# Gate and up weights in runs of 2 KB: another cut of two weight matrices into the same pieces

## The chip, the core and the metric

The kernel runs on one core of a Trainium2 chip. The metric is the device time of one execution in microseconds (us). Three runs of the kernel before gave 324.64, 325.95 and 326.41 us, a median of 325.95.

## The reference, cut to what matters

```python
x = A_x                                             # 2048 x 512, bf16
x = x + _A_ref(_layernorm(x), A_wqkv, A_wo)         # 32 heads of 16, causal window of 256
x = x + _B_ref(_layernorm(x), B_w_r, B_w_gate, B_w_up, B_w_down)
x = x + _A_ref(_layernorm(x), A_wqkv, A_wo)
x = x + _B_ref(_layernorm(x), B_w_r, B_w_gate, B_w_up, B_w_down)

def _B_ref(x, w_r, w_gate, w_up, w_down):           # C = 1: one row of 2048 goes through the MLP
    r = x @ w_r
    idx = argsort(-r)[:, :1]
    x_sel = x[idx]                                  # 1 x 512
    y = (silu(x_sel @ w_gate) * (x_sel @ w_up)) @ w_down        # 512 -> 1792 -> 512
    return x + scatter(idx, y * sigmoid(r[idx]))
```

So each of the two layers has an attention over 2048 rows and an MLP of a single row. For that row the gate and up products are matrix times vector: 512 x 1792 weights each, of which 128 x 128 blocks are loaded into TensorE as weights and multiplied with one column.

## The kernel before, in words

The kernel is a list of operations (`S.add`, `S.dma`), each with an engine, the tiles it reads and writes, an assumed duration and a priority. `Sched.schedule` (line 189) plays this list through once, at build time, and so fixes the order of every engine's instructions. The chip then runs the five orders with semaphores between them; an engine never overtakes in its own order.

Two rules of the planner matter here. The attention's matmuls on TensorE (PE) carry a `seq` and run in the order of that number. All other PE operations are "loose" (line 248): one of them is put ahead of the next fixed operation when it can start no later than that one and has a lower priority number, or when it fits before it. And a DMA is taken to land a fixed while after its issue, plus its bytes and the bytes of the DMAs issued before it (lines 355 to 357); the planner does not know into how many runs a DMA falls. SyncE (SP) issues nearly all DMAs, in one order.

The sequence is cut into 16 tiles of 128 rows per layer. While the attention of a layer runs, the row for the MLP is chosen from the first 11 tiles (layer 0) or 10 tiles (layer 1) (`select`), fetched from DRAM and normed into `XST`, a tile of 128 x 4: row `4p + kc` of the 512 sits in partition `p`, column `kc`. Then come, in both layers:

- `load_mlp` (line 1277): 21 pieces of weights of 256 KB, 1024 elements per partition. Pieces 0, 2, ... 12 are gate, 1, 3, ... 13 are up, 14 to 20 are down. Each piece goes to a home (`spots`, lines 1511 and 1528) in a tile that is free for the moment: `MW`, `XI`, `QT` and others. In layer 0 the homes of pieces 11 to 17 are those of pieces 2 to 9, so these loads wait until a gate-up step has read the old piece (line 1523): pieces 11 and 12 after step 1, 13 and 14 after step 2, 15 and 16 after step 3, 17 after step 4. A load's priority is that of its step.
- `mlp_gu` (line 1316): seven gate-up steps. Step `c` takes pieces `2c` and `2c + 1` and makes blocks `2c` and `2c + 1` of the 14 blocks of 128 outputs, for gate and up: 32 matmuls of one column, each block a sum over four `kc` that opens and closes by itself. All steps write one PSUM bank. Their priorities fall with `c` in layer 0 (`gu0` = -5.834 per step) and rise with `c` in layer 1 (`gu1` = 2.222); no step depends on another, but steps 5 and 6 of layer 0 need pieces 11 to 13.
- `mlp_act` (line 1339) and `mlp_down` (line 1350): silu, the product, and 56 matmuls with the down pieces; then the row is put back by a DMA. In layer 0 the second layer's loads of the rows wait for that.

The gate and up weights lie in DRAM as 512 rows of 1792. Before, a piece is 256 columns of all rows: per partition four runs of 256 elements (512 bytes), each of another row. A home in `QT` holds a piece as four runs of 256 elements that lie apart; in every other home the piece's 1024 elements of a partition are one run.

Of the kernel before, what the change touches and what calls it, by code (L numbers as in the profile page):

```python
# [505 lines left out]
FULL, HALF = 1, 2  # L506
# [19 lines left out]
class Builder:  # L526
# [750 lines left out]
    def load_mlp(self, c, where, at):  # L1277

        S = self.S
        buf, keys = self.home(where)  # L1280
        wk = ["piece%s%d" % where] if where[0] == "w" else keys
        deps = set()
        if where[0] == "w":
            for x in keys:
                deps.add(S.last_writer[x])
                deps.update(S.readers.get(x, ()))
        deps.add(S.groups[-1].ops[0])
        if c < 14:
            n = 256 * (c // 2)
            src = (self.B_w_gate, self.B_w_up)[c % 2].rearrange("(p kc) n -> p kc n", p=128)[:, :, n:n + 256]  # L1290
            dst = buf if where[0] == "qt" else buf.rearrange("p (kc n) -> p kc n", kc=4)
        else:
            n = 2 * (c - 14)
            src = self.B_w_down.rearrange("(j p) n -> p j n", p=128)[:, n:n + 2, :]
            dst = buf.rearrange("p (j n) -> p j n", j=2)
        S.dma("sp", lambda e: e.dma_start(dst, src), writes=wk, nbytes=256 * 1024, name="ld_mw", prio=at, extra_deps=deps)
        self.pieces[c] = (dst, wk)
# [18 lines left out]
    def mlp_gu(self, L, c, at, ate):  # L1316

        S = self.S
        S.base = at
        NF = self.NF  # L1320
        if c == 0:
            self.GUG = S.group("x")
        G = self.GUG
        ps = [self.pieces[2 * c + u] for u in range(2)]

        def gu(e):
            r = None
            for u in range(2):
                for j in range(2):
                    k = NF * u + 2 * c + j  # L1330
                    for kc in range(4):
                        r = e.matmul(self.PS[:, G.bank, k:k + 1], lhsT=ps[u][0][:, kc, 128 * j:128 * j + 128], rhs=self.XST[:, kc:kc + 1],  # L1332
                                     start=(kc == 0), stop=(kc == 3))
            return r
        S.add("pe", gu, reads=["xst"] + ps[0][1] + ps[1][1], banks=[0], group=G, dur=16 * 27 + 150, instrs=32, mode=FULL, name="gateup", prio=at + POS["gp%d" % L])
        if c == 6:
            S.add("dve", lambda e: e.tensor_copy(out=self.GU[:], in_=self.PS[:, G.bank, 0:2 * NF]), banks=[0], group=G, writes=["gu"], dur=110, name="evgu", prio=ate)

# [1213 lines left out]
```

## Time and profile before

| | |
|---|---|
| median of 3 runs | 325.95 us (324.64 to 326.41) |
| profiled execution | 326.61 us, its span 324.9 us |
| PE busy | 305.1 us (94%), 7315 matmuls |
| PE weight loads | 222.0 us (68%) |
| DVE, ACT, POOL busy | 272.4, 272.9, 143.7 us |
| DMA queue of SP and ACT | 44.78 MB in the span, 58.3% of 16 engines |

Times of rows are microseconds from the span's start unless marked ns. PE is TensorE's matmuls, PEld its weight loads, which run beside them; DVE is VectorE, ACT ScalarE, POOL GpSimd, SPq the DMA issues of SyncE. The busy share of PE is an upper bound, since the ends of pipelined matmuls are modelled. The granted TensorE clock is 0.998 of full speed over the span.

### The profile page before, as it was taken

To read this page: it belongs to the slowest core of one execution; us is meant where nothing else is said; L and a number is where in the kernel's file an instruction comes from. 1 tells how busy PE (TensorE), PEld (TensorE's weight loads), DVE (VectorE), ACT (ScalarE), POOL (GpSimd) and SP (SyncE) were. 2 spreads that over 40 slices of the span, in tenths; PEclk is the share of its full clock that TensorE was granted. 3 is DMA by queue.
4 is the path that set the end of the run, shared out by engine and by line. 5 is a ranking of instruction groups with operands and counts; after the bars stand their busy time and mean duration, and the time that the engine had idled before them with its cause. 6 is when DMAs were issued, how large, how long until landed. Compare 5 with 4: busy or idle time off the path is not lost.

```text
span 324.9 us, 16648 instructions
## 1 busy us (share of the span) xinstructions
PE 305.1 (94%) x7315; PEld 222.0 (68%) x7377; DVE 272.4 (84%) x728; ACT 272.9 (84%) x313; POOL 143.7 (44%) x322
## 2 busy tenths in 40 slices
PE   8978999999999999999998999999999999989995
PEld 3735677677766776777776567677677767767773
DVE  7987998999797878799877899879788687888793
ACT  8599999999889899988357999898989998999621
POOL 6280348688656170414733457351304222313441
PEclk9999999999999999999999999999999999999999
DMA  7826312627447968736694477989967546554502
GB/s 240 272 78 131 71 34 68 166 44 166 79 126 185 152 172 128 171 75 178 197 152 106 124 155 198 214 211 211 272 167 216 151 146 135 168 121 103 118 18 58
DMA packets 86546, 46.95 MB, mean 145 GB/s; under 512 B 52420, under 2 KB 80708, under 8 KB 86468
## 3 DMA queue, kind: packets, MB, share of 16 engines
q1 hardware_dynamic: 85380, 44.78, 58.3%
q8 instruction: 59, 0.97, 1.3%
q10 hardware_dynamic: 1088, 1.05, 1.0%
q14 instruction: 19, 0.16, 0.3%
HBM read 24.78 MB, written 13.43 MB: 118 GB/s over the span
## 4 chain that ended last, share of the span: by engine, by line
PE 77%; ACT 11%; DVE 4%; issue 3%; DMA 3%; SPq 0%; POOL 0%; POOLq 0%
PE PS L981 16%; PE PS L839 15%; PE PS L861 15%; PE PS L1047 14%; ACT PT L959 11%; PE PS L1052 9%; PE PS L1013 3%; DMA vd<-VN 2%; PE PS L666 2%; PE PS L1332 1%; PE PS L1408 1%; DVE KBD L931 1%; PE PS L1372 1%; DVE ON L1071 1%; DMA VBD<-vd 1%
## 5 line engine op out<-in xcount | busy, mean ns | idle before, releaser
L959 ACT ACTIVATE PT<-PS 128x1024 bf16<-128x1024 f32 (+4 forms) x284 | 257.6, 989 | 34.1 <-PE PS L981 33.1
L981 PE MATMUL PS<-QT,KBD 64*128 64x256 bf16 (+4 forms) x1024 | 82.3, 265 | 1.9 <-issue 0.9
L1137 POOL TENSOR_TENSOR XR<-XR,MHALF 128x1 f32<-128x1 f32 x32 | 18.9, 589 | 139.2 <-DVE XR L1136 133.8
L861 PE MATMUL PS<-XNT,WQKV 128*128 128x256 bf16 x480 | 62.6, 274 | 1.6 <-DVE ON L1071 0.8
L981 PEld LDWEIGHTS PS<-QT,KBD 64*128 64x128 bf16 x1024 | 35.6, 94 | 36.2 <-issue 14.2
L1047 PE MATMUL PS<-VBD,PT 128*128 128x68 bf16 x1488 | 55.2, 196 | 1.7 <-DMA VBD<-vd 1.3
L861 PEld LDWEIGHTS PS<-XNT,WQKV 128*128 128x128 bf16 x480 | 42.6, 98 | 17.5 <-issue 7.1
L1047 PEld LDWEIGHTS PS<-VBD,PT 128*128 128x128 bf16 x1488 | 50.8, 97 | 5.5 <-issue 3.9
L1052 PEld LDWEIGHTS PS<-VBD,PT 64*128 64x128 bf16 x2784 | 40.4, 93 | 3.4 <-ACT PT L959 1.6
L1052 PE MATMUL PS<-VBD,PT 64*128 64x34 bf16 x2784 | 41.6, 175 | 0.9 <-ACT PT L959 0.5
L992 DVE TENSOR_TENSOR PT<-PT,MSK 128x512 bf16<-128x512 bf16 x64 | 28.4, 444 | 7.9 <-ACT PT L959 7.6
L839 PE MATMUL PS<-WQKV,XNT 128*128 128x512 bf16 x99 | 26.4, 379 | 4.9 <-issue 2.9
L1071 DVE TENSOR_TENSOR ON<-PS,RD 128x256 bf16<-128x256 f32 x64 | 26.9, 420 | 1.5
L874 DVE CAST KTN<-PS 128x512 bf16<-128x512 f32 x30 | 20.6, 687 | 8.2 <-PE PS L861 8.2
L839 PE MATMUL PS<-WO,OT 128*128 128x512 bf16 x90 | 24.3, 379 | 3.3 <-issue 2.5
L931 DVE TENSOR_SCALAR KBD<-KTN,M 128x1024 bf16<-128x1024 bf16 x60 | 26.3, 488 | 0.4
L1069 DVE RECIPROCAL RD<-PS 128x16 f32<-128x16 f32 x64 | 16.1, 252 | 10.4 <-PE PS L1052 7.6
L1138 DVE SCALAR_TENSOR_TENSOR JUNK<-XR,WR 128x512 bf16<-128x512 f32 x32 | 23.6, 738 | 0.7
L923 DVE CAST VN<-PS 128x512 bf16<-128x512 f32 x30 | 20.6, 685 | 4.0 <-PE PS L839 3.9
L874 DVE CAST QT<-PS 128x512 bf16<-128x512 f32 x28 | 19.2, 684 | 5.0 <-PE PS L861 4.6
L1134 DVE BATCH_NORM_STATS2 ST6M<-XR 128x6 f32<-128x512 f32 x32 | 21.8, 681 | 0.0
L839 PEld LDWEIGHTS PS<-WQKV,XNT 128*128 128x128 bf16 x128 | 10.6, 97 | 13.5 <-issue 2.7
(149 smaller groups left out, 343.2 us busy)
## 6 DMA issues: line engine op xcount, KB each, us to landing
scr<-XR SPq DMA_DIRECT2D x12, 516.0 KB, 3.7
vd<-VN SPq DMA_DIRECT2D x16, 272.0 KB, 3.9
VBD<-vd SPq DMA_DIRECT2D x128, 34.0 KB, 2.8
XR<-scr SPq DMA_DIRECT2D x8, 512.0 KB, 4.6
XI<-in_B_w_down_dram SPq DMA_DIRECT2D x7, 256.0 KB, 3.2
out_dram<-OUTB SPq DMA_DIRECT2D x7, 256.0 KB, 4.2
XI<-in_A_x_dram SPq DMA_DIRECT2D x6, 256.0 KB, 7.4
MW<-in_B_w_up_dram SPq DMA_DIRECT2D x6, 256.0 KB, 5.2
```

The source lines that it names most:

```text
L839: r = e.matmul(self.PS[:, G.bank, 0:n], lhsT=lhs(j), rhs=rhs(j), start=(j == 0), stop=(j == 3))
L861: r = e.matmul(self.PS[:, G.bank, 256 * u:256 * u + 256], lhsT=self.WQKV[:, j, c:c + 128], rhs=XNT[:, kb, 2 * h:2 * h + 2, j, :], start=(u ...
L874: S.add("dve", lambda e: e.tensor_copy(out=dst, in_=src[:, G.bank, :].rearrange("p (s t) -> p s t", s=2)), banks=[0], group=G, writes=keys ...
L931: S.add("dve", lambda e, h=h: e.tensor_scalar(out=self.KBD[:, k2, :, :, 32 * h:32 * h + 32].rearrange("p s b k -> p (s b) k"), in0=src, sc ...
L959: return e.activation(out=out, in_=i, func=ACTF.Exp, scale=0.25)
L981: r = e.matmul(self.PS[:, G.bank + x, W * u:W * u + n], lhsT=self.KBD[rows, k2, s, 4 * (T % 2) + b, :], rhs=self.QT[rows, s, q0:q0 + n], s ...
L992: S.add("dve", lambda e: e.tensor_tensor(out=P, in0=P, in1=m, op=ALU.mult), reads=["msk"], writes=["pt%d_%d" % ((4 * T + b) % 12, 2 * sp + ...
L1047: r = e.matmul(o, lhsT=self.PT[:, c:c + 128], rhs=self.VBD[:, v, kb % 4, :, 2 * s + a, :], start=isfirst and kb == blocks[0] and g == 0, s ...
L1052: r = e.matmul(self.PS[:, G.bank + x, 34 * g:34 * g + 34], lhsT=self.PT[rows, c:c + 128], rhs=self.VBD[rows, v, kb % 4, 2 * x:2 * x + 2, 2 ...
L1071: S.add("dve", lambda e: e.tensor_tensor(out=o, in0=acc()[:, :, :, 0:16], in1=rd.unsqueeze(3).broadcast_to([128, 2, 8, 16]), op=ALU.mult), ...
L1134: S.add("dve", lambda e: e.bn_stats(out=self.ST6M[:, km, :], in_=x), reads=[xk], writes=["st6m#%d" % km], dur=600, name="bnst2", prio=ag)
L1138: S.add("dve", lambda e: e.scalar_tensor_tensor(out=self.JUNK[:], in0=x, scalar=1.0, in1=self.WR16[:], op0=ALU.mult, op1=ALU.mult, accum_o ...
```

## The change

A piece now is, per partition, a run of 1024 elements out of the 7168 that the four rows of a partition make together (they are adjacent in DRAM). With 14 blocks of 128 columns in a row, piece number `c` (of gate or of up) holds the blocks `8c` to `8c + 7` of the 56 blocks of all four rows, so that a step has eight blocks of gate and eight of up, of one `kc` or of two. The number of matmuls, their shapes, the homes and the bytes stay the same.

The sums over `kc` now run across steps. So one matmul of a layer, the first of step 0, opens the bank (`start`), all others add to it or write where nothing was written yet, and each step depends on the step before it (`extra_deps`).

```diff
         if c < 14:
-            n = 256 * (c // 2)
-            src = (self.B_w_gate, self.B_w_up)[c % 2].rearrange("(p kc) n -> p kc n", p=128)[:, :, n:n + 256]
+            n = 1024 * (c // 2)
+            src = (self.B_w_gate, self.B_w_up)[c % 2].rearrange("(p kc) n -> p (kc n)", p=128)[:, n:n + 1024].rearrange("p (a n) -> p a n", a=4)
             dst = buf if where[0] == "qt" else buf.rearrange("p (kc n) -> p kc n", kc=4)
...
             for u in range(2):
-                for j in range(2):
-                    k = NF * u + 2 * c + j
-                    for kc in range(4):
-                        r = e.matmul(self.PS[:, G.bank, k:k + 1], lhsT=ps[u][0][:, kc, 128 * j:128 * j + 128], rhs=self.XST[:, kc:kc + 1],
-                                     start=(kc == 0), stop=(kc == 3))
+                for j in range(8):
+                    kc, k = divmod(8 * c + j, NF)
+                    k += NF * u
+                    r = e.matmul(self.PS[:, G.bank, k:k + 1], lhsT=ps[u][0][:, j // 2, 128 * (j % 2):128 * (j % 2) + 128], rhs=self.XST[:, kc:kc + 1],
+                                 start=(c == 0 and u == 0 and j == 0), stop=(c == 6 and u == 1 and j == 7), skip_group_check=True)
             return r
-        S.add("pe", gu, reads=["xst"] + ps[0][1] + ps[1][1], banks=[0], group=G, dur=16 * 27 + 150, instrs=32, mode=FULL, name="gateup", prio=at + POS["gp%d" % L])
+        self.gu_ix = S.add("pe", gu, reads=["xst"] + ps[0][1] + ps[1][1], banks=[0], group=G, dur=16 * 27 + 150, instrs=32, mode=FULL, name="gateup", prio=at + POS["gp%d" % L],
+                           extra_deps=[self.gu_ix] if c else [])
```

## Rows read from the trace of the kernel before

**Rows 1.** Page, part 4: chain that ended last, shares of the span by engine.
```profile
PE 77%; ACT 11%; DVE 4%; issue 3%; DMA 3%; SPq 0%; POOL 0%; POOLq 0%
```

**Rows 2.** Waits of PE, whole span: engine, line, releaser: total us, times, longest us.
```profile
PE PS L1047 <- DMA VBD<-vd: 1.3, 1, 1.3
```

**Rows 3.** Chain that ended last, whole span and from 296: start, us, what.
```profile
22.49 2.13 DMA VBD<-vd
...
296.60 0.38 PE PS L1332 x16
```

**Rows 4.** The same chain, stretch of 150 to 200.
```profile
155.49 1.98 PE PS L1332 x80
...
160.63 0.98 PE PS L861 x8
...
164.99 0.88 PE PS L1332 x32
...
171.24 0.85 issue
...
174.69 9.31 ACT PT L959 x10
```

**Rows 5.** Stretches: PE, PEld, DVE, ACT, POOL busy, clock, DMA share, GB/s.
```profile
170.00:172.20 2.20, 1.35 (x79) 1.06 (x72) 1.34 (x5) 1.78 (x2) 1.91 (x5) 1.00 0.21 36
...
210.00:240.00 30.00, 29.29 (x743) 21.57 (x749) 23.86 (x59) 27.41 (x30) 10.73 (x24) 1.00 1.02 235
```

**Rows 6.** Line 1332, gate-up matmuls: ns min/median/max, first and last start us.
```profile
L1332 PE MATMUL PS<-XST,MW x88: 163/163/177, 156.1 to 298.8; 128*128 128x1 bf16 x88
...
L1332 PE MATMUL PS<-XST,XI x72: 163/163/178, 155.3 to 313.6; 128*128 128x1 bf16 x72
...
L1332 PE MATMUL PS<-XST,QT x64: 163/163/178, 155.5 to 313.8; 128*128 128x1 bf16 x64
```

**Rows 7.** Timeline of PE's weight loads, 150 to 175: start, us, what.
```profile
155.25 0.32 PEld L1332 LDWEIGHTS PS<-XST,XI 128*128 128x128 bf16 x8 [0.26 <-issue]
...
156.10 0.87 PEld L1332 LDWEIGHTS PS<-XST,MW 128*128 128x128 bf16 x32
156.90 0.47 PEld L1332 LDWEIGHTS PS<-XST,QT 128*128 128x128 bf16 x16
...
164.92 0.27 PEld L1332 LDWEIGHTS PS<-XST,QT 128*128 128x128 bf16 x8 [0.21 <-issue]
165.12 0.67 PEld L1332 LDWEIGHTS PS<-XST,MW 128*128 128x128 bf16 x24
```

**Rows 8.** Timeline of SP's DMA issues, 130 to 161: start, us, what.
```profile
143.00 0.33 SPq L950 DMA_DIRECT2D VBD<-vd  x1
...
155.95 1.43 SPq L1296 DMA_DIRECT2D XI<-in_B_w_down_dram  x3
157.44 0.58 SPq L1296 DMA_DIRECT2D MW<-in_B_w_up_dram  x1
...
159.33 0.82 SPq L1296 DMA_DIRECT2D MW<-in_B_w_gate_dram  x1
160.25 1.03 SPq L950 DMA_DIRECT2D VBD<-vd  x2
```

**Rows 9.** Line 1296, issues of the weight loads: ns min/median/max, first and last start.
```profile
L1296 SPq DMA_DIRECT2D XI<-in_B_w_down_dram x7: 390/403/1123, 143.8 to 248.3; - x7
...
L1296 SPq DMA_DIRECT2D MW<-in_B_w_gate_dram x5: 571/598/820, 92.0 to 207.6; - x5
L1296 SPq DMA_DIRECT2D QT<-in_B_w_up_dram x5: 546/594/1354, 101.2 to 243.7; - x5
```

**Rows 10.** DMA issues in 155 to 161: count, KB each, median us to landing.
```profile
XI<-in_B_w_down_dram SPq DMA_DIRECT2D x3, 256.0 KB, 3.0
MW<-in_B_w_up_dram SPq DMA_DIRECT2D x2, 256.0 KB, 5.4
```

**Rows 11.** DMA view, whole span: packets by size.
```profile
DMA packets 86546, 46.95 MB, mean 145 GB/s; under 512 B 52420, under 2 KB 80708, under 8 KB 86468
```

## The prediction, made before the result was known

> **What bounds the kernel now.** I read the chain of waits first. Three quarters of it are TensorE's own instructions, a ninth is ScalarE, and DMA has 3% [rows 1]. Then the waits of TensorE: there are three for a DMA in the whole trace, all in the start-up; the one shown lies on the chain at 22 us [rows 2, 3], long before the first gate or up weight is asked for at 92.0 us [rows 9]. From there to the end no matmul waits for a transfer. Even where the DMA share is highest, 1.02 with 235 GB/s in 210 to 240 us, PE is busy 29.29 of 30 us [rows 5]. So the reader is to see a kernel that is bound by the order and the number of PE's instructions, with DMA beside it.
>
> The stretch that the change touches most is 155 to 175 us, between the layers. There the chain runs over the gate-up steps themselves: 80 matmuls in 1.98 us, then 32 in 0.88 us. It has one hole of 0.85 us at 171.24 in which PE waited for nothing that the profile shows, and at 174.69 it goes over to ScalarE, which had been waiting for scores [rows 4]. What is lost or won by PE before 174.69 therefore reaches the end of the kernel one to one, until another slack swallows it.
>
> **The change part by part.** The sum is made against the profiled execution, 326.61 us with a span of 324.9; the median of the runs is 0.66 us below it, and I take that off at the end.
>
> *PE's work.* Gate-up is 88 + 72 + 64 = 224 matmuls of one column in both layers, 163 ns each in the median [rows 6], and by the diff there are 224 of the same shape after (7 steps of 16, two layers). The opening of the bank is a flag on a matmul, no instruction. Cost: 0.
>
> *The transfers.* 28 pieces are loaded. A piece of four runs costs SP 0.57 to 0.60 us, a down piece, which is two runs of 1 KB per partition, 0.40 us [rows 9], a quarter of V with 128 runs 0.33 us [rows 8]. A piece of 128 runs should cost 0.33 to 0.40 us, so SP gains 0.17 to 0.27 us per piece. Eight of the 28 have their home in `QT`, where the written side stays four runs of 512 bytes; if the shorter side counts, those gain nothing, and SP saves 20 x 0.17 = 3.4 us at the least, 28 x 0.27 = 7.6 us at the most. None of it is on the path: the first layer's loads that need no freed home are issued from 92.0 us on for a step at 155.49 [rows 4, 9], and the second layer's end at 243.7 us for a step at 296.60 [rows 3, 9]. The cover is 52 us there. What could be quicker behind a shorter queue are V loads and transposes, and PE waits for none of them now. Value: 0; bounds below.
>
> The Trainium skill (DMA: Bandwidth & Descriptors, Specifications) puts the smallest transfer at full rate at 512 bytes, by which the old runs were already good and the change would not move more bytes per microsecond. The same page (Why small descriptors are slow) counts three cycles for each packet on top of one per 32 bytes: an estimate from it is 4 x 19 = 76 cycles before and 67 after, 12% less. The rows mix this with the queue: in the same stretch three down pieces landed in 3.0 us and two up pieces, queued behind them, in 5.4 [rows 10]. By either the sum stays, since nothing waits; by the first, the slower rival below is likelier.
>
> *The chain of steps.* In layer 1 the steps' priorities already rise with the step, so nothing moves. In layer 0 they fall, and the order of homes in the trace says so: `XI` and `QT` first (step 4), then `XI` (3), `MW` (2 and 1), `QT` (0), then after 8 us `QT` and `MW` (5 and 6) [rows 7]. The chain turns the five round: 0, 1, 2, 3, 4. As a burst they cost what they cost now, 1.98 us. What moves is what waits for them: SP's loads into freed homes. Now the first, the three into `XI`, leave at 155.95, when step 4 has read, and the last, piece 12 into `MW`, at 159.33 [rows 8]. After, the first is piece 11, when step 1 has read: 32 matmuls of 24.7 ns after 155.49, that is 156.28, and about 0.06 us for the signal as now, so 156.34. Behind it SP takes by priority 13, then 15, 17, 16, 14, and 12 last. All seven go 0.39 us later at the start, but three of them are of the new kind and 0.2 us cheaper each, so that the V loads behind them, now at 160.25 [rows 8], leave within 0.3 us of that, and piece 12 no later than now.
>
> *Step 5 moves forward.* It needs pieces 10 and 11 only. By its own rule the planner counts piece 11 as landed 4.35 us after its issue (0.62 for the issue, 0.3, 0.93 for 256 KB, 2.4, and 0.1 for the signal; this says where it puts the step, not what the chip takes), that is at about 160.7 on the trace's scale. Step 5 has a lower priority number than any fixed operation there, so it goes into PE's order at that place, just ahead of or behind the projection at 160.63 [rows 4], four microseconds before its place of now. Step 6 waits for piece 12 and stays near 165. So the pair of steps, 32 matmuls in 0.88 us, is split. Against the rate in the burst (32 x 24.7 ns = 0.79 us) a group that stands alone costs 0.09 us more; one more group costs +0.09 us. Downstream, `mlp_act` and the down matmuls hang on step 6 and keep their place, or slip by a few matmuls: 0 to 0.4 us (half of the 0.85 us that a group of such small matmuls now takes at 165), and I take 0.
>
> *The hole of 0.85 us.* It stands in the stretch 170 to 172.2, in which the DMA share is 0.21 and 36 GB/s move [rows 5]. A queue that is nearly empty is not made quicker by fewer packets, so I leave the hole where it is: 0, with -0.85 as its other end.
>
> Sum: 0 + 0 + 0.09 + 0 + 0 = +0.1 us on 326.61, or 326.05 on the scale of the median: I say 326.0. What a measurement of this kernel can tell from no change is about 0.5%, 1.6 us: under 324.3 is faster, over 327.6 slower.
>
> **The rivals.**
>
> *Faster: the emptier DMA queues reach PE after all.* PE's instructions come over DMA too, and if such fetches stood behind packets of the weights, the small pauses of PE in the loaded stretches would shrink. Speaking for it: a pause with no cause shown. Against it: that pause falls into an empty stretch, and the fullest one has PE idle for only 0.71 of 30 us [rows 5]. Price at most: the 0.85, and 0.71/30 over the 53 us in which the second layer's pieces are loaded, 1.25 us; together -2.1, so 323.9 us. The Trainium skill (Runtime: NRT & Kernel Launch, Instruction fetch mechanics) says that an engine fetches blocks of 256 instructions over a DMA queue of its own, mostly hidden; the row at 170 us agrees that weights are not what it waits for.
>
> *Slower: PE stands before step 5.* PE's order is fixed, so if piece 11 has not landed when step 5 is up, the projection and the scores behind it all wait, and ScalarE after them. It decides at 160.63 - 156.34 = 4.3 us after the issue. For it: the two up pieces into `MW` landed after 5.4 us in just this stretch; then PE stands 5.4 + 156.34 - 160.63 = 1.1 us. Against it: those stood behind three others, while piece 11 would be the first in its queue, and the three at the head now took 3.0 us [rows 10]. Step 5 would also set 32 small instructions right behind a dense stretch of PE, where a second hole like that at 171.24 can open, 0.85 us. Price: 1.1 + 0.85 + 0.09 = +2.0, so 328.0 us.
>
> *The runs don't become 2 KB.* The source is written as four times 256 elements in the diff. If that is how it is carried out, the packets stay what they are, only the chain acts, and the time is the forecast's, 326.0, with piece 11 a little later.
>
> **How the numbers follow.** No change, with the case that the runs stay short: 0.56, its own range 325.1 to 327.3. The faster rival 0.20, at 323.9. The slower rival 0.17, at 328.0. The planner plays the whole list again, and an order tipped elsewhere by step 5's place can go either way: 0.02 faster, 0.05 slower. So faster 0.22, same 0.56, slower 0.22, and a range that leaves out the outer part of both rivals, 324.1 to 328.1.
>
> **What would show it.** Packets: 14,336 of the 86,546 [rows 11] are runs of the 28 pieces (512 each); all in 2 KB would leave 75,794, the `QT` pieces excepted 78,866, and 86,546 would mean that nothing was joined. The issue of a piece into `MW` or `XI` should take 0.33 to 0.40 us. In layer 0 the homes should come in the order `QT`, `MW`, `XI`, `QT`, and 16 of the matmuls should start at about 160.5, without idle time of PE ahead of them that ends with a DMA. The hole near 171 should still be there. I would be wrong if that hole goes or a second one comes, if step 5 waits, or if the second layer's stretches, where only the loads differ, change their length.

## The result, and the profile after

The changed kernel takes 329.0 us in the median of 12 runs (326.36 to 331.46), the one before 326.48 beside it (324.45 to 327.81, 12 runs): a ratio of 1.0068, 95% interval 1.0038 to 1.0097. The ratio leaves out one run of after, the 331.46, that lies over 1.5% above its fastest. The change is slower, by 0.7%, where none was forecast; 329.0 lies above the range.

What was said of the loads came out. The page of the kernel after has the packets of the case in which the `QT` pieces stay short, 78,866 against the 86,546 of before [rows 11]:

```profile
DMA packets 78866, 46.95 MB, mean 143 GB/s; under 512 B 52420, under 2 KB 70468, under 8 KB 78788
```

The place where the time went shows in the chain of waits of after, from the burst of gate-up steps on (start, us, what). It answers to [rows 4]. (A gate-up step is 16 matmuls, eight of gate and eight of up, so the 80 are five steps; the 32 in the words on the kernel count the weight loads too.)

```profile
154.48 1.98 PE PS L1332 x80
...
157.07 1.23 PE PS L861 x8
...
158.47 1.39 PE PS L1052 x96
159.85 0.52 PE PS L1332 x16
160.38 1.79 issue
162.16 0.56 PE PS L981 x8
162.72 1.82 PE PS L861 x8
164.54 0.22 issue
164.76 1.48 PE PS L839 x3
...
166.52 1.47 PE PS L1047 x24
...
169.20 0.48 PE PS L1332 x16
...
175.25 0.98 PE PS L861 x8
```

Step 5 (159.85) starts about where the prediction put it, and PE does not wait for it. Behind it PE stands still for 1.79 us with no releaser. And the projection, 0.98 us at 160.63 in [rows 4], takes 1.82 us. The windows of after show why (PE busy, clock, DMA share, GB/s): the granted clock fell to half, 1.2 GHz, even before the hole.

```profile
154.00:158.00 4.00, 3.82 (x94) 0.96 0.58 137
158.00:162.00 4.00, 2.38 (x118) 0.50 1.00 320
162.00:166.00 4.00, 3.61 (x19) 0.50 1.41 179
166.00:170.00 4.00, 4.00 (x71) 0.76 0.00 0
```

Before has a short hole at the same place, which the rows ahead of the prediction do not list. Its row in the chain of before, with that of the projection behind the down matmuls:

```profile
161.61 0.29 issue
...
172.48 0.98 PE PS L861 x8
```

From the burst's start to that projection (at 172.48 before, at 175.25 after) it is 16.99 us before and 20.77 after, +3.78. By the rows: the hole +1.50; instructions stretched by the half clock +2.58 (L861 +0.25 and +0.84, L1052 +0.17, L839 +0.67, L981 +0.07, L1047 +0.58); the pause at 164.54 +0.22; step 5 alone +0.12 (0.52 + 0.48 - 0.88); the split of a group in the down steps +0.09; and the hole of 0.85 at 171 is gone. That makes 3.66. From there to the end the two agree within 0.3 us; up to the burst after was 1.01 us ahead, so the spans differ by 2.6 and not by 3.8. The burst starts anywhere between 153.8 and 155.6 in the profiles of this document, so I read nothing into that. And this execution has the lowest mean clock of after's 12 (0.984; the others have 0.988 to 0.995), so the half clock is likely to cost less than 2.58 in most of them.

SP's timeline of after says what else moved (start, us, issue), against [rows 8]:

```profile
152.56 2.83 SPq L950 DMA_DIRECT2D VBD<-vd  x4
155.49 0.38 SPq L1187 DMA_DIRECT2D scr<-XR  x1
155.96 0.86 SPq L1296 DMA_DIRECT2D MW<-in_B_w_up_dram  x2
156.92 1.49 SPq L1296 DMA_DIRECT2D XI<-in_B_w_down_dram  x3
```

The store of a row tile to `scr`, 258 KB, now leaves ahead of the seven loads. Before, it left behind them:

```profile
163.85 0.43 SPq L1187 DMA_DIRECT2D scr<-XR  x1
```

### The profile page after: what moved, and what is told of

The parts are those of the page before. It is cut to its first block, busy times and chain, and to the rows that moved or that the text cites. A ratio compares the mean times of both kernels' runs of the same rounds, so it can differ in the third digit from the quotient of the medians.

```text
span 327.5 us, 16648 instructions
## 1 busy us (share of the span) xinstructions
PE 307.1 (94%) x7315; PEld 223.4 (68%) x7377; DVE 272.1 (83%) x728; ACT 272.6 (83%) x313; POOL 143.7 (44%) x322
## 2 busy tenths in 40 slices
DMA packets 78866, 46.95 MB, mean 143 GB/s; under 512 B 52420, under 2 KB 70468, under 8 KB 78788
## 4 chain that ended last, share of the span: by engine, by line
PE 77%; ACT 13%; DVE 5%; issue 3%
PE PS L861 16%; PE PS L981 16%; PE PS L839 15%; PE PS L1047 14%; ACT PT L959 12%; PE PS L1052 9%; PE PS L1013 3%; PE PS L1332 1%; PE PS L1409 1%; DVE KBD L931 1%; PE PS L1373 1%; DVE VBD L680 1%; PE PS L1108 1%; DVE ST L772 1%; DVE ON L1071 1%
## 5 line engine op out<-in xcount | busy, mean ns | idle before, releaser
L981 PE MATMUL PS<-QT,KBD 64*128 64x256 bf16 (+4 forms) x1024 | 82.4, 266 | 3.1 <-issue 1.8
L861 PE MATMUL PS<-XNT,WQKV 128*128 128x256 bf16 x480 | 63.6, 277 | 1.6 <-DVE ON L1071 0.8
L981 PEld LDWEIGHTS PS<-QT,KBD 64*128 64x128 bf16 x1024 | 35.8, 94 | 38.2 <-issue 15.0
L1047 PE MATMUL PS<-VBD,PT 128*128 128x68 bf16 x1488 | 55.8, 197 | 1.3 <-ACT PT L959 1.1
L861 PEld LDWEIGHTS PS<-XNT,WQKV 128*128 128x128 bf16 x480 | 43.0, 98 | 17.9 <-issue 7.3
L1047 PEld LDWEIGHTS PS<-VBD,PT 128*128 128x128 bf16 x1488 | 51.4, 98 | 5.2 <-issue 3.5
L1052 PEld LDWEIGHTS PS<-VBD,PT 64*128 64x128 bf16 x2784 | 40.7, 93 | 3.4 <-ACT PT L959 1.6
L1052 PE MATMUL PS<-VBD,PT 64*128 64x34 bf16 x2784 | 42.0, 175 | 0.9 <-ACT PT L959 0.5
L839 PE MATMUL PS<-WQKV,XNT 128*128 128x512 bf16 x99 | 26.5, 379 | 4.1 <-issue 2.7
L839 PE MATMUL PS<-WO,OT 128*128 128x512 bf16 x90 | 25.0, 387 | 3.3 <-issue 2.5
L839 PEld LDWEIGHTS PS<-WQKV,XNT 128*128 128x128 bf16 x128 | 10.7, 98 | 12.8 <-issue 2.7
```

What stands on the lines that cost most here:

```text
L839: r = e.matmul(self.PS[:, G.bank, 0:n], lhsT=lhs(j), rhs=rhs(j), start=(j == 0), stop=(j == 3))
L861: r = e.matmul(self.PS[:, G.bank, 256 * u:256 * u + 256], lhsT=self.WQKV[:, j, c:c + 128], rhs=XNT[:, kb, 2 * h:2 * h + 2, j, :], start=(u ...
L981: r = e.matmul(self.PS[:, G.bank + x, W * u:W * u + n], lhsT=self.KBD[rows, k2, s, 4 * (T % 2) + b, :], rhs=self.QT[rows, s, q0:q0 + n], s ...
L1047: r = e.matmul(o, lhsT=self.PT[:, c:c + 128], rhs=self.VBD[:, v, kb % 4, :, 2 * s + a, :], start=isfirst and kb == blocks[0] and g == 0, s ...
L1052: r = e.matmul(self.PS[:, G.bank + x, 34 * g:34 * g + 34], lhsT=self.PT[rows, c:c + 128], rhs=self.VBD[rows, v, kb % 4, 2 * x:2 * x + 2, 2 ...
```

## The experiments

Each ran beside the kernel before on its chip; the figure after it is the ratio to that, with a 95% interval. Diffs are against after where nothing else is said, with lines left out at `...`. In the order in which they were formed, the theories were: the long runs load the chip in another way (T); or the chain's order does (O), by the store that moves ahead of the loads (S) or by step 5's early place (D); and for the hole itself, that PE waits for the transfer of its next instructions, which stands behind the weights' traffic (theory F in the earlier expectations, A in the later ones), or that it is a wait of the instruction behind step 5 (B).

**after_again**: no edit.

> The changed kernel once more, for a second profile. Its first profile lost 3.8 us to the one of before between the gate-up burst and the point where ScalarE takes over (19.2 us before, 23.0 after): a hole of PE of 1.79 us right behind step 5 at 160.4, and a stretch at half the granted clock from about 157.9 to 169. Both theories below expect a ratio of about 1.007 here. If the hole belongs to the program, it stands at the same instruction in this profile, at 1.5 to 2.0 us. If the half clock belongs to it too, the granted clock is 0.50 in 162 to 166 again; if the clock falls by chance, it may be 1.00 here and the hole still there.

1.0080 [1.0046, 1.0113], hole 2.00 us at 160.93. The result repeats. The clock is at half in two stretches here, from the end of the burst to 160.0, and from 163.4, half a microsecond behind the hole; between them it is full.

**chain_512**: the pieces of before, and of the change the chain alone (the blocks of before need no chain for their sums). The diff is against before.

```diff
-        S.add("pe", gu, ...)
+        self.gu_ix = S.add("pe", gu, ..., extra_deps=[self.gu_ix] if c else [])
```

> The kernel before with the chain of steps alone: pieces and packets of before (four runs of 512 bytes), order of all instructions as in the changed kernel. Theory O (order): step 5, moved ahead of a dense stretch's end, makes PE run out of instructions, whatever the runs are: ratio to before 1.005 to 1.010, hole behind step 5 of 1.5 us or more. Theory T (traffic): the pieces of 2 KB runs leave SP faster and fill the DMA engines just when PE's instructions are fetched: ratio 0.998 to 1.002, hole behind step 5 under 0.5 us.

1.0072 [1.0032, 1.0112], hole 2.22 us. The short runs with the chain have the whole loss, so the long runs aren't needed for it. In its profile step 5 did wait for piece 11 as well, which left behind the store (chain, start, us, what):

```profile
156.47 4.24 DMA MW<-in_B_w_up_dram
160.71 0.05 issue
160.75 0.55 PE PS L1332 x16
161.31 2.22 issue
```

**runs_old_order**, and a second time **runs_old_again**: the pieces of 2 KB without the chain; the bank is opened by the step that comes first in layer 0, so PE and SP keep the order of before.

```diff
-                                 start=(c == 0 and u == 0 and j == 0), ...
+                                 start=(c == (0 if L else 4) and u == 0 and j == 0), ...
-                           extra_deps=[self.gu_ix] if c else [])
+                           extra_deps=[])
```

> The runs of 2 KB alone: pieces and steps as in the changed kernel, but no chain; the bank is opened by the step that comes first in the old order (step 4 in layer 0), and PE's order is that of the kernel before, step for step. Theory O: ratio 0.996 to 1.002, no hole at 160, the old one of about 0.85 us near 171 as before. Theory T: ratio 1.004 to 1.010, with a hole or a slow fetch between 156 and 165 although the order is the old one.

> The kernel of runs_old_order unchanged (the eight-block pieces in 2 KB runs, no chain, step order of before), a second time. If it does beat before by the 0.27% that the first measurement gave: ratio 0.995 to 0.999. If that was chance: 0.999 to 1.003. The hole after matmul 3482: 0.2 to 1.4 us.

0.9973 [0.9946, 1.0000], then 1.0005 [0.9976, 1.0033]. With the order kept, 2 KB runs are worth nothing that can be told: the first figure was chance, at least in part. The profile of the first has a hole of 1.35 us all the same (chain), at the full clock, that of the second one of 0.44 with the clock at half behind the burst, so one profile's hole doesn't give a kernel's time. The first:

```profile
160.92 1.35 issue
162.27 0.81 PE PS L839 x3
...
171.44 0.48 issue
```

**step5_late**: step 5 also waits for pieces 12 and 13, and so stays with step 6.

```diff
+        more = [k for y in (12, 13) for k in self.pieces[y][1]] if L == 0 and c == 5 else []
-        ... reads=["xst"] + ps[0][1] + ps[1][1], ...
+        ... reads=["xst"] + ps[0][1] + ps[1][1] + more, ...
```

> The changed kernel with one thing more: step 5 of layer 0 also waits for pieces 12 and 13, so that it stands beside step 6 again as before; the turned order of steps 0 to 4, the loads and the runs are those of the changed kernel. Theory O, with the place of step 5 as its cause: hole at 160 gone, ratio 0.998 to 1.003. Theory T, or the turned order of the burst as the cause: ratio 1.005 to 1.009 and a hole near 160 still.

1.0041 [1.0005, 1.0077], about half of after_again's excess, though the intervals overlap and the hole stays (1.93 us, now ahead of L839).

**store_back**: after, but the store waits for step 5 and so goes behind the loads.

```diff
+            if L == 0 and st == (11, 1):
+                self.st11 = ix              # ix: the store's index
...
+        if L == 0 and c == 5:
+            S.ops[self.st11].deps.add(self.gu_ix)
```

> The first look showed a hole of PE that ends at 162 to 163.5 in every variant, and begins where PE has used up its instructions (160.4 to 161.3); what differs is when it ends. In the changed kernel SP also issues the store of one XR tile (258 KB) just ahead of the seven weight loads, at 155.49, where it stood at 163.85 before: SP had become free while it waits for step 1. Here the store waits for step 5, so that it stands behind the loads again; PE's order is that of the changed kernel. Theory S (the store ahead of the loads makes the traffic that the fetch of PE's instructions stands in): ratio 1.000 to 1.004, hole behind step 5 under 1.0 us. Theory D (place of step 5 and density of instructions alone): ratio 1.006 to 1.010, hole 1.7 to 2.2 us.

1.0026 [0.9993, 1.0059], hole 1.43 us. The ratio is the one that theory S gives, the hole lies between the two theories. By its interval this edit alone can be told neither from before nor, surely, from after.

**both_undone**: these two edits together.

> After, with the store behind step 5 (store_back) and step 5 behind pieces 12 and 13 (step5_late). If the two shares add up (store 0.5%, early step 0.4% of after's 0.8%): ratio 0.997 to 1.001, hole 0.3 to 1.4 us. If both lengthen one and the same hole only where the other is there: ratio 1.002 to 1.004, no better than the better of the two alone.

1.0003 [0.9973, 1.0034]: the loss is gone, with the long runs, the chain and the turned burst still in. So the store ahead of the loads and the early step 5 are together what the change costs; how much each costs alone is not resolved. The chain of waits of this kernel has, at the old place, ahead of L839:

```profile
162.50 0.17 issue
```

PE was at half clock behind the burst in this profile (the first L861 x8 took 1.82 us) and came to this place 5.19 us behind the burst's end, where before needed 4.14; the short hole is in part PE's own lateness.

**old_order_store**: runs_old_order with one more store of 256 KB, to a spare tensor, right ahead of the seven loads.

> The other side of it: the runs of 2 KB in the old order (which ran at 0.997), with one more store of 256 KB, out of a constant tile into a spare DRAM tensor, issued just ahead of the seven loads; all other orders unchanged. Theory S: ratio 1.001 to 1.006, hole near 161 longer than the 1.35 us of the profile without it, by 0.5 to 1.0 us. Theory D: ratio 0.995 to 1.000, hole as without it.

1.0016 [0.9986, 1.0046], against 0.9973 and 1.0005 without it. The first pair pointed at the store, the repeat doesn't: inconclusive. In its profile no long hole stands there, and the clock is 0.57 in 158 to 162.

**short_down** and **pad128** were meant to cut pieces 14 to 17, and to put 128 empty instructions ahead of PE's program.

```diff
-PAD = 0
+PAD = 128
```

> The changed kernel with the four down pieces among the seven loads of layer 0 (14 to 17) cut to an eighth of their columns; the rest of these pieces is left out, so this part of the first MLP isn't computed. Issues, order and semaphores stay. About 0.9 MB less goes through the DMA engines in 156 to 165 us. Theory F (the hole is the fetch of PE's next instructions behind the weights' traffic, whatever put it there): hole behind step 5 under 0.6 us, no stretch at half clock, ratio 0.994 to 1.000. Theory D: hole 1.7 to 2.2 us as in the changed kernel, ratio 1.006 to 1.010.

> The changed kernel with 128 empty instructions at the head of PE's order, where PE waits for its first operand; nothing else is moved. If PE's instructions come in blocks, every block's end moves by 128 instructions, half of what I take a block to hold from 16.4 KB in each of the 59 packets of the instruction queue. Theory F: the hole is no longer behind step 5 at 160 to 163 but gone or elsewhere, ratio 0.997 to 1.003 (the head itself may cost up to 1 us). Theory D, in a form in which dense instructions alone starve PE: hole behind step 5 as before, ratio 1.006 to 1.012.

Neither edit reached the program: the flag was off again by the time the loads were made (46.95 MB and 78,866 packets, as in after), and the empty instructions are not in it (59 packets of instructions and the hole at the same count of matmuls as without them). So they say nothing of either theory and are two more repeats of after: 1.0068 [1.0036, 1.0101], hole 1.57, and 1.0084 [1.0047, 1.0121], hole 2.41. The next two put the questions again.

**thin**: store_back, with pieces 11 to 17 of layer 0 loaded in 16 of 128 partitions (that part of the MLP is left out).

```diff
+        part = 16 if 11 <= c <= 17 and at < self.NT else 128
-        ... e.dma_start(dst, src), ...
+        ... e.dma_start(dst[0:part], src[0:part]), ...
```

> The kernel of store_back (after, with row tile 11's store behind step 5) in which layer 0's pieces 11 to 17 load 16 of their 128 partitions; the other partitions keep older weights, so their part of layer 0's MLP is left out. TensorE's order and the issues' order are store_back's. Theory A (behind the burst TensorE reaches the end of its block of instructions, and the 16 KB transfer of the next block stands behind the weights' traffic): with 0.22 MB instead of 1.75 MB to move, that transfer starts within 1.5 us of the burst's end instead of 2.4 to 4.8, the hole of 1.43 us behind step 5 shrinks to 0.5 us or less, and the ratio falls from store_back's 1.003 to 0.996 to 1.000. Theory B (the hole is a wait of the instruction behind step 5 that has nothing to do with the traffic): a hole of 1.3 us or more stays, ratio 1.001 to 1.005.

0.9994 [0.9962, 1.0026]. Behind step 5 the hole is 0.08 us, in the same order of instructions as after (chain, then a window):

```profile
159.86 0.52 PE PS L1335 x16
160.38 0.08 issue
160.47 0.56 PE PS L981 x8
```

```profile
160.00:162.00 2.00, 1.92 (x29) 0.50 0.27 50
```

With some 50 GB/s in the queues, where after had 320 in 158 to 162, the hole is gone, and the clock is at half nonetheless. Traffic lengthens the hole; it isn't needed for the half clock. Two things limit this: the ratio's interval overlaps that of store_back, and PE, at half clock here and at the full one in store_back's profile, reached the place 0.5 us later behind the burst (3.98 against 3.45 us), which hides that much of a hole of 1.43.

**shift60**, and a second profile **shift60_again**: after with 64 matmuls of one column for the first 4 of the warm-up, so that everything behind stands 60 matmuls later in PE's program.

```diff
-                for _ in range(4):
+                for _ in range(64 if first else 0):
+                    r = e.matmul(... JUNK, one column ...)
+                for _ in range(0 if first else 4):
```

> After, with the first group of warm-up matmuls at the start (4 of 512 columns) replaced by 64 of one column: 60 more matmuls stand ahead of everything else in TensorE's program, at about the same time. Theory A: the hole stands at a place of the program's memory, not behind a step: it again comes after some 3482 recorded matmuls (as in before and after), so 60 matmuls earlier in the order, inside the 96 matmuls of L1052 ahead of step 5. Theory B: it stays directly behind step 5. In both the hole is 1.3 to 2.4 us long; ratio 1.004 to 1.010 (A: down to 1.000 if the step before it then hides some of it).

> A second profile of shift60. Theory A: again no hole behind step 5, since the transfer starts within the burst, ahead of the weights' loads. If a hole of 1.3 us or more stands behind step 5 this time, the place of the block's end was not what removed it.

1.0044 [1.0013, 1.0075]. In both profiles no hole stands behind step 5, nor 60 matmuls ahead of it, where theory A had it. The second one's timeline of PE (start, us, operation, idle time ahead) goes from step 5 to the scores without a pause, and has a hole in layer 1 that after does not, nor the first profile of shift60 (326.17 us, the fastest of its 12 executions):

```profile
160.80 0.34 PE L1334 MATMUL PS<-XST,MW 128*128 128x1 bf16 x8
161.07 0.37 PE L983 MATMUL PS<-QT,KBD 64*128 64x128 bf16 x8
...
310.08 0.44 PE L983 MATMUL PS<-QT,KBD 64*128 64x128 bf16 x5 [1.90 <-issue]
```

So the hole belongs to a place in PE's program, not to step 5. With the hole gone, PE came to step 6 ahead of piece 12, which landed 6.0 and 7.2 us after its issue, and waited for it in both profiles (waits of PE: total us, times, longest), as it does not in before or after:

```profile
PE PS L1334 <- DMA MW<-in_B_w_gate_dram: 1.1, 1, 1.1
```

```profile
PE PS L1334 <- DMA MW<-in_B_w_gate_dram: 0.8, 1, 0.8
```

In these two profiles about half of what the hole had cost after (1.79 and 2.00 us) was lost there again.

**old_shift60**, **old_shift20**, **old_shift30**: runs_old_order with 60, 20 and 30 more matmuls at the start.

> runs_old_order with the 60 more matmuls at the start as in shift60. Theory A: the 16 KB transfer moves ahead of the weights' traffic, starts within the burst, and no hole over 0.3 us stands where runs_old_order had 1.35 us (behind the second L861 x8); by the profile alone that is worth 1.0 us, ratio 0.993 to 0.998, if the moved ends of the other blocks of instructions cost nothing. If they cost what shift60 lost elsewhere (1.0044 with no hole in its profile): 1.000 to 1.004.

> runs_old_order with 20 more matmuls at the start (24 of one column for 4 of 512) instead of 60. Theory A: the block's end behind the burst moves 20 matmuls ahead, from behind the second L861 x8 to behind the 84th of the 96 of L1052, and the transfer is asked for while the burst runs: hole there 0.5 us or less, and in layer 1 the block's end falls 11 matmuls into L1052's 96 (with 60 it fell behind them, with holes of 1.6 and 1.9 us near 310 in two profiles), hole there 0.5 us or less. Ratio 0.993 to 0.999. Rival: the holes only change place, ratio 1.000 to 1.004.

> The same with 30 more matmuls: the block's end behind the burst falls behind the 74th of L1052's 96, in layer 1 directly ahead of L1052's 96. Theory A: no hole over 0.5 us at either place, ratio 0.993 to 0.999; rival: ratio 1.000 to 1.004, with a hole over 1 us elsewhere.

1.0035 [1.0000, 1.0070], 1.0067 [1.0033, 1.0101], 1.0055 [1.0021, 1.0089]. No hole in layer 0 with 60 (in layer 1 one of 1.63 us, up to 309.84, instead); with 20 and 30 none over 0.8 us anywhere behind the first 30 us of the profile, and yet slower. The expectation that time follows the holes failed here; why is open. The profile with 20 says little on it: it is of the fastest of that kernel's 12 executions, 326.45 us at full clock, below the median of before. Five of these kernels' 36 runs have a mean clock of 0.997 or more, about half of those of before beside them.

**before_again**: a second profile of before.

> A second profile of before. If the length of the hole after matmul 3482 is what tells before from after: 0.2 to 0.9 us here, clock 1.00 in the 10 us behind the burst. If it is 1.3 us or more, the hole is no difference between the two, and the time went elsewhere.

No hole near 161 in PE's timeline, where 0.2 us at the least was expected, but the half clock is there in before too, for some 3 us (timeline, then window). The expectation of clock 1.00 was wrong:

```profile
157.81 1.75 PE L861 MATMUL PS<-XNT,WQKV 128*128 128x256 bf16 x8
...
161.42 1.05 PE L861 MATMUL PS<-XNT,WQKV 128*128 128x256 bf16 x8
162.33 1.02 PE L839 MATMUL PS<-WO,OT 128*128 128x512 bf16 x4
```

```profile
158.00:160.00 2.00, 2.00 (x44) 0.50 1.00 326
```

**What the hole waits for.** Count the matmuls that the records have from the start to the hole, by windows: before, then after.

```profile
0.00:161.61 161.61, 151.44 (x3482) 108.84 (x3513) 138.77 (x358) 140.20 (x162) 85.36 (x191) 1.00 0.56 136
```

```profile
0.00:160.38 160.38, 150.37 (x3482) 0.99 0.57 136
```

It is the same number, 3482, in before, after_again, chain_512, runs_old_order and step5_late too, although step 5 is among them only in some (the profiles that miss no records have 3512). Close to it falls the start of one packet of 16 KB in the queue q8, which carries instructions: 0.97 MB in the span. I take them for PE's, whose 14,692 recorded instructions are the only program near that size (DVE has 728). The DMA view has it in these windows of before, after and thin (queue, kind: packets, MB, share), 158.7 to 159.0, 159.6 to 159.9 and 158.1 to 158.4:

```profile
q8 instruction: 1, 0.02, 19.3%
```

```profile
q8 instruction: 1, 0.02, 21.1%
```

```profile
q8 instruction: 1, 0.02, 18.3%
```

By the trace's records of this packet (us, to 0.1):

| kernel | burst's last matmul | packet starts | hole ends | hole |
|---|---|---|---|---|
| thin | 156.4 | 158.2 | 160.5 | 0.08 |
| before | 157.5 | 158.8 | 161.9 | 0.29 |
| both_undone | 157.3 | 160.4 | 162.7 | 0.17 |
| store_back | 156.1 | 158.5 | 161.0 | 1.43 |
| runs_old_order | 156.8 | 159.6 | 162.3 | 1.35 |
| after | 156.5 | 159.7 | 162.2 | 1.79 |
| step5_late | 157.0 | 160.2 | 163.1 | 1.93 |
| after_again | 156.4 | 160.3 | 162.9 | 2.00 |

The hole ends 2.3 to 3.1 us after that packet starts, in each of these profiles, wherever the program then stands; and the packet starts 1.3 to 3.9 us behind the burst's end. In shift60 and its repeat it started at 155.5 and 155.2, within the burst, ahead of the seven loads: no hole.

The hole of 0.85 us at 171.24 in before [rows 4] is of the same kind. It stands 252 recorded matmuls behind the first (3734), and a packet of 16 KB starts 2.65 us ahead of its end, at 169.4 (DMA view, 169.3 to 169.6), though only 36 GB/s moved in 170 to 172.2 [rows 5]:

```profile
q8 instruction: 1, 0.02, 23.9%
```

Three things make a hole long, then. *The packet itself*: some 2.3 us pass from its start to the hole's end even in thin, and it starts 1.8 us behind the burst there, with hardly any weights in the queues. *The traffic*: with the store ahead of the loads in the chain's order the packet starts 3.2 to 4.9 us behind the burst's end (after, after_again, short_down, pad128, chain_512, step5_late), without it 1.3 to 3.3 (both profiles of before and of runs_old_order, store_back, both_undone). It spreads by over 1 us within one kernel, and old_order_store, which has a store ahead too, has 2.5. *PE's own pace*: at the full clock it reaches the place 4.14 us behind the burst's end in before, and 3.45 with step 5 there in place of the scores and the projection (store_back); at half clock later, with less of a hole.

That PE waits for its next block of instructions is what the count, thin and the shifts show together. That the store makes this block late rests on the packets' starts and on both_undone; it is likely, and not isolated.

Two things stay open. One is how the loss of 2.5 us divides between hole and clock: every one of the 12 runs of after had a mean clock of 0.995 or less (and 35 of the 36 in after_again, short_down and pad128), while about half of those of before beside after_again had 0.997 or more, and thin and runs_old_order show that either comes without the other. A bound can be read from the runs of equal clock, 0.992 to 0.995: after took 329.88, 329.39 and 329.22 us in the mean of these (after_again, short_down, pad128; 17 runs), before beside them 327.65 and 328.09. So 1.1 to 2.2 us are left where the clock is the same, of 2.4 to 3.2 between the medians. And a hole may bring a second stretch of half clock: in after_again, short_down and pad128 one begins within 0.6 us of the hole's end, in chain_512 and store_back the only one behind the burst begins within 0.9 of it; in runs_old_order and step5_late none does. The other open thing is the 0.4 to 0.7% of the shifted kernels, of which step 6's wait in shift60 is the one part that a profile shows. The planner's order is the same in them, fitted to other ends of the blocks; that this costs the rest is a guess. Nothing tried beats the kernel before; runs_old_order equals it.

## Why the prediction was wrong

The steps that failed are "Step 5 moves forward", priced at +0.09, and "The chain of steps", in which what moves was said to be SP's loads alone, at no cost to PE. The runs show in their place 0.7% for the two together: 1.0068 and 1.0080 with both in, 1.0003 with both taken back (both_undone). The term that the sum has at nothing is the wait of PE for its own instructions, 0.29 us before and 1.79 after behind the burst.

The kernel that I read has this term. Where the planner plays PE's operations it counts their instructions in blocks of 256, and lets no block begin before a time that is reckoned from the block ahead of it and from the DMAs still to land (lines 342 to 348; `FETCH` is 3000 ns, line 493; `...` for lines left out):

```python
left = op.instrs + 1
while count + left >= 256:
    ...
    entered = at_ + FETCH + 0.8 * max(0.0, fifo - at_)
```

I named two rules of the planner and passed over this third one. An order that is turned, with a store moved ahead of seven loads, had to be held against it.

- **PE's work, 0: right.** 224 matmuls of one column, and 80 of them again in 1.98 us.
- **The transfers, 0: right.** The issue of a gate piece into `MW` fell from 598 ns in the median [rows 9] to 430, that of a piece into `QT` from 594 to 396, though its packets stayed short; gate pieces into `XI` stayed near 0.58 us. The two behind the store took 0.86 together. runs_old_order and its repeat put the worth at nothing.
- **The chain of steps: order right, SP's list wrong.** The homes came as `QT`, `MW`, `XI`, `QT`, and the first V loads behind the pieces left 4.99 us after the burst's start (159.47 - 154.48), against 4.76 before [rows 4, 8]. But I listed only what waits for the five steps. The planner had the first load ready with step 4, the first of the old burst; in the new one the first is ready with step 1, the second of the burst, and SP, free at 155.39, has the store to issue in between. So the store went first, and piece 11 left 1.48 us after the burst's start and not 0.85. The working named the queue and missed what was ready in it.
- **Step 5: place right, price wrong.** It started without waiting (the up pieces 11, which it needs, and 13 landed after 3.8 us in the median), so the slower rival's stall ahead of step 5 did not occur in after; in chain_512 it did, 0.8 us. The group alone cost 0.12 at half clock, and 0.08 in store_back at the full one, as priced. What the price left out is that 16 small matmuls right behind L1052's 96 bring PE sooner to the end of its block of instructions, by 0.69 us at the full clock (4.14 against 3.45), just when 0.26 MB more are in the queues.
- **The hole of 0.85 at 171.24, left at 0: wrong by its other end.** It is gone in after. The slower rival had the thought of "a second hole" behind step 5 and gave it the size of that one; it was the earlier hole, of 0.29 us, that grew. That the rival's 328.0 lies nearest to the measured 329.0 is in part luck: 1.1 of its 2.0 us are the stall, which did not come.
- **The faster rival had the mechanism with the sign turned.** I looked for a late fetch at 171, in an empty stretch, and concluded that weights are not what it waits for. That was right of the weights and wrong of the fetch: the hole there ends 2.65 us after a packet of instructions starts, as the others do. At 161, with 320 GB/s in the window, the traffic comes on top. Fewer packets of weights did not make the packet start sooner, even without the store: 2.8 and 3.3 us behind the burst in runs_old_order and its repeat, 1.3 and 2.7 in before and its repeat.
- **The clock was not in the sum.** [rows 5] show 1.00 for their stretches, and I took it for the state of the stage. It falls to half behind the burst in other executions of before too.

## What to carry to other kernels

Pauses of an engine without a releaser are worth a count: if they come after the same number of instructions in two orders, look whether a packet of instructions starts ahead of their end, and what lies in the DMA queues at that moment. An empty queue does not rule such a wait out. Before an order is turned, list what the DMA-issuing engine could issue in the time that it is freed earlier, not only what waits for the moved step. Read what the planner counts before judging what it leaves out. A program that has been fitted closely can lose more by a move of some instructions than the edit could bring, so test the data layout and the order apart.

## What the runs showed of the hardware

- Instructions come in packets of 16 KB (59 in the trace, 0.97 MB), and PE can be made to wait for one: up to 2.4 us. The Trainium skill (Runtime: NRT & Kernel Launch, Instruction fetch mechanics) has blocks of 16 KiB, 256 instructions, fetched by a queue of the engine's own, and calls the cost mostly hidden. The size of the packets agrees; hidden it is in thin, 0.08 us, and not in after, 1.79.
- Behind a burst of 80 one-column matmuls the granted clock went from 2.4 to 1.2 GHz in 12 of the 19 profiles, between 0.2 us ahead of the burst's end and 1.2 us behind it, and stayed there for 3 to 10 us; in two (chain_512, store_back) it did so some 6 us behind the burst, near the end of a hole; in five it stayed at 2.4 GHz, three of them of kernels whose other profile has it (before, runs_old_order, shift60). The same L861 x8 takes 0.98 or 1.82 us by it.
